# One attention-and-MLP kernel: TensorE's order fixed in the attention steps, maxima in own columns, every third step's scores in the ring of sums

## Chip, core and metric

The kernel runs on one core of a Trainium2 chip. The metric is the device time of one execution in microseconds (us); the median of several runs is given. TensorE multiplies matrices, VectorE, ScalarE and GpSimd work elementwise or along rows, SyncE issues transfers. Matrix products land in PSUM, eight banks in which each tile here fills one or part of one.

## The reference

The attention with random features, whose sizes are batch 8, heads 8, tokens 576, head width 64, 128 features:

```python
def phi(x):
    proj = np.einsum('bhsd,md->bhsm', x, omega)
    sq = np.sum(x * x, axis=-1, keepdims=True) / 2.0
    h = proj - sq
    h = h - np.max(h, axis=-1, keepdims=True)
    return np.exp(h) / np.sqrt(m)
q_p, k_p = (phi(q_s), phi(k_s))
kv = np.einsum('bhsm,bhsd->bhmd', k_p, v)
z = np.sum(k_p, axis=2)
num = np.einsum('bhsm,bhmd->bhsd', q_p, kv)
den = np.einsum('bhsm,bhm->bhs', q_p, z)[..., None] + 1e-06
return (num / den).astype(np.float32)
```

Its output, heads side by side, is the input x of a token mixing `u = x + (xT @ U @ V)T` and of an MLP `u + relu(u @ w_ch1) @ w_ch2` with widths 512 and 2048.

## The kernel before

**Attention.** The work is cut into 16 units, each two batches by two heads, and a unit's tokens into 9 tiles of 128. A round works on the keys of one unit and on the queries of an earlier one (both of its parts are queries or keys at the ends), and a round has 9 steps, one for each tile. A step goes through stages that are spread over the loop's passes (`DELAY`): 2 passes after its start it is projected, at 3 its maxima are taken, at 4 the exponentials run and are used, at 5 the transposed exponentials are copied out of PSUM, at 6 the query products are made, at 7 the result is divided. So in each pass TensorE meets stages of several steps. These are:

- **Projection** (`Step.project`): six matmuls, three for each part, into a bank of scores `p_p`. The ring `p_p` has two banks, so that step n+2 writes where step n was.
- **Maxima** (`peak`): one reduction on VectorE over the four score blocks, into a small tile `nm` of a ring of two.
- **Exponentials** (`exp`): four on ScalarE, with `nm` as the bias, first the two of the queries (`exp1`), then the two of the keys, into `e`, a ring of two.
- **Key product** (`Keys.use`): two products of `e` with the values, added up over the round in a bank `p_kv` or `p_m`.
- **Transposition** (`Queries.use`): two, of the queries' `e` against the identity, into `p_q`, a ring of two; `copy` moves them to `eT` on VectorE or ScalarE in turn.
- **Query product** (`Queries.combine`): two products of `eT` with the finished `kv`, into a tile of sums `p_n`, a ring of two banks. A tile holds two steps (step 4 has one alone). In `finish`, VectorE adds the small constant (L603), takes reciprocals (L604) and multiplies (L618), after which the slot is free.

Once per four units a mixer (`mixing`) puts its matmuls `py` and `ph` between these, and now and then a piece of a weight (`decoding`) or of the MLP's input (`ahead`) is prepared.

**What sets the order.** The kernel is recorded in program order and a scheduler then orders each engine's instructions by modelled times. Instructions inside `tc.keep_in_program_order(...)` keep their order among themselves on their engine. Before, in the attention steps these are on TensorE the key products

```python
tc.keep_in_program_order(nc.tensor.matmul(
    o, e[:, j, :], w, start=(s == 0 and j == 0), stop=(s == NT - 1), skip_group_check=True
))
```

while projections, transpositions and query products (`nc.tensor.matmul(...)` alone) go where the scheduler puts them. Everything after the attention steps, the MLP, is kept in program order.

## Time and profile before

| | |
|---|---|
| median of 3 runs | 1040.44 us (1040.01 to 1041.32) |
| profiled execution | 1040.75 us |
| its span, first to last instruction | 1039.0 us |
| TensorE matmuls, weight loads busy | 1030.3, 988.6 us |
| VectorE, ScalarE, GpSimd busy | 780.7, 588.7, 464.9 us |
| granted TensorE clock, mean | 0.999 |

The table is of the profiled execution but for its first line. A matmul's end is modelled and its time overlaps with that of the next; weight loads, which run one ahead of the matmuls, are a row of their own (PEld). The starts of weight loads tell best how long a piece of TensorE's work takes.

### The profile page before, as it was taken

To read this page: it belongs to the slowest core of one execution; us is meant where nothing else is said; L and a number is where in the kernel's file an instruction comes from. 1 tells how busy PE (TensorE), PEld (TensorE's weight loads), DVE (VectorE), ACT (ScalarE), POOL (GpSimd) and SP (SyncE) were. 2 spreads that over 40 slices of the span, in tenths; PEclk is the share of its full clock that TensorE was granted. 3 is DMA by queue.
4 is the path that set the end of the run, shared out by engine and by line. 5 is a ranking of instruction groups with operands and counts; after the bars stand their busy time and mean duration, and the time that the engine had idled before them with its cause. 6 is when DMAs were issued, how large, how long until landed. Compare 5 with 4: busy or idle time off the path is not lost.

```text
span 1039.0 us, 19292 instructions
## 1 busy us (share of the span) xinstructions
PE 1030.3 (99%) x6487; PEld 988.6 (95%) x6487; DVE 780.7 (75%) x1549; ACT 588.7 (57%) x1481; POOL 464.9 (45%) x419
## 2 busy tenths in 40 slices
PE   9999999999999999999999999999999999999998
PEld 7999999999989999999898999999999999999998
DVE  3898998998987776487678666886678676875556
ACT  4989889899865654454443534543455334543441
POOL 2356547567344654578773423322333223322231
PEclk9999999999999999999999999999999999999999
DMA  6899889788315474389868999989999899889887
GB/s 153 149 170 147 164 177 169 166 172 139 97 51 171 145 177 77 112 276 300 285 241 278 309 294 303 282 270 281 288 277 284 270 287 277 270 261 273 262 235 181
DMA packets 372883, 226.44 MB, mean 218 GB/s; under 512 B 307760, under 2 KB 324912, under 8 KB 372784
## 3 DMA queue, kind: packets, MB, share of 16 engines
q1 hardware_dynamic: 369712, 224.26, 80.3%
q10 hardware_dynamic: 3072, 0.95, 0.4%
q8 instruction: 52, 0.85, 0.4%
q14 instruction: 47, 0.39, 0.1%
HBM read 176.91 MB, written 48.23 MB: 217 GB/s over the span
## 4 chain that ended last, share of the span: by engine, by line
PE 82%; DVE 2%; DMA 1%; ACT 1%; POOL 0%; issue 0%; DVEq 0%; POOLq 0%; ACTq 0%
PE p_s L1124 27%; PE p_c L1414 12%; PE p_o L1414 6%; PE p_p L1095 6%; PE p_n L1247 4%; PE p_q L1247 4%; PE p_r L1414 3%; PE p_n L593 3%; PE p_kv L479 2%; PE p_kv L1247 2%; PE p_m L1247 2%; PE p_p L635 2%; PE p_q L573 2%; PE p_p L636 2%; PE p_p L637 2%; PE py L338 1%
## 5 line engine op out<-in xcount | busy, mean ns | idle before, releaser
L1124 PE MATMUL p_s<-ux,wx 128*128 128x384 f32 x1680 | 332.3, 335 | 0.2 <-ACT near L1194 0.2
L1124 PEld LDWEIGHTS p_s<-ux,wx 128*128 128x128 f32 x1680 | 295.7, 188 | 4.0 <-ACT near L1194 0.7
L650 ACT ACTIVATE e<-p_p,nm 128x128 f32<-128x128 f32 x540 | 156.8, 389 | 22.1 <-DVE nm L643 11.7
L905 POOL TENSOR_TENSOR near<-b,near 128x384 f32<-128x384 f32 x32 | 42.3, 1323 | 263.3 <-DVE near L1173 247.7
L1414 PE MATMUL p_c<-t,wy 128*128 128x384 f32 x756 | 151.1, 334 | 0.3 <-DMA wy<-w2x_dram 0.3
L1414 PEld LDWEIGHTS p_c<-t,wy 128*128 128x128 f32 x756 | 132.8, 188 | 0.6 <-DMA wy<-w2x_dram 0.6
L428 POOL TENSOR_TENSOR xl<-xT,xh 128x384 fp32r<-128x384 f32 x90 | 91.5, 1038 | 83.9 <-ACT xh L424 58.0
L643 DVE TENSOR_REDUCE nm<-p_p 128x4 f32<-128x512 f32 x135 | 91.9, 681 | 15.4 <-PE p_p L637 8.2
L635 PE MATMUL p_p<-omh,xh 128*128 128x256 f32 x270 | 85.9, 318 | 0.6 <-ACT e L650 0.6
L905 DVE TENSOR_TENSOR near<-p_s,near 128x384 f32<-128x384 f32 x88 | 48.8, 555 | 48.5 <-PE p_s L1124 42.2
L905 POOL TENSOR_TENSOR t<-near,t 128x768 fp32r<-128x768 f32 x32 | 59.3, 1853 | 41.0 <-ACT t L1183 41.0
L1414 PE MATMUL p_o<-t,wy 128*128 128x384 f32 x384 | 76.9, 334 | 0.0
L637 PE MATMUL p_p<-omh,xl 128*128 128x256 f32 x270 | 75.8, 281 | 0.0
L636 PE MATMUL p_p<-oml,xh 128*128 128x256 f32 x270 | 75.8, 281 | 0.0
L593 PE MATMUL p_n<-kv,eT 128*128 128x65 f32 x512 | 71.1, 268 | 0.1
L593 PEld LDWEIGHTS p_n<-kv,eT 128*128 128x128 f32 x512 | 67.1, 192 | 2.4 <-DVE eT L578 0.4
L1414 PEld LDWEIGHTS p_o<-t,wy 128*128 128x128 f32 x384 | 67.5, 188 | 0.0
L1095 PE MATMUL p_p<-ux,wx 128*128 128x384 f32 x360 | 66.4, 335 | 0.0
L905 DVE TENSOR_TENSOR w1f<-p_c,w1f 128x384 f32<-128x384 f32 x78 | 43.4, 557 | 29.8 <-PE p_c L1414 29.5
L1095 PEld LDWEIGHTS p_p<-ux,wx 128*128 128x128 f32 x360 | 63.4, 188 | 1.5
L573 PE MATMUL p_q<-ident,e 128*128 128x128 f32 x288 | 60.5, 277 | 0.8 <-ACT e L650 0.7
L479 PE MATMUL p_kv<-vt,e 128*128 128x65 f32 x416 | 57.6, 261 | 0.0
(202 smaller groups left out, 2263.1 us busy)
## 6 DMA issues: line engine op xcount, KB each, us to landing
wx<-wx_dram SPq DMA_DIRECT2D x112, 512.0 KB, 4.5
wy<-w2x_dram SPq DMA_DIRECT2D x112, 512.0 KB, 5.0
raw<-in_moe_w_ch_dram SPq DMA_DIRECT2D x32, 512.0 KB, 4.1
wx_dram<-wx SPq DMA_DIRECT2D x56, 256.0 KB, 2.6
u_dram<-x SPq DMA_DIRECT2D x36, 256.0 KB, 2.3
qt<-in_q_dram SPq DMA_DIRECT2D x120, 72.0 KB, 3.0
uraw<-u_dram SPq DMA_DIRECT2D x80, 96.0 KB, 5.4
kt<-in_k_dram SPq DMA_DIRECT2D x52, 144.0 KB, 4.8
```

The lines of the kernel that those rows point to most:

```text
L428: rest.tensor_tensor(out=self.xl[-1], in0=self.turned, in1=f32(self.xh[-1]), op=ALU.subtract)
L593: nc.tensor.matmul(pn[:, h, :], eT[:, h, :], kv[:, h, s // 5, :], start=True, stop=True)
L635: nc.tensor.matmul(o, part.xh[g][:, ts], oh, start=True, stop=False)
L636: nc.tensor.matmul(o, part.xh[g][:, ts], ol, start=False, stop=False)
L637: nc.tensor.matmul(o, part.xl[g][:, ts], oh, start=False, stop=True)
L643: nc.vector.tensor_reduce(out=self.nm[:, :n], in_=self.pp[:, :n], axis=AX.X, op=ALU.max, negate=True)
L650: nc.scalar.activation(out=self.e[:, j, :], in_=self.pp[:, j, :], func=AF.Exp, bias=self.nm[:, j : j + 1])
L905: keep(engine.tensor_tensor(out=out, in0=a, in1=b, op=op))
L1095: keep(nc.tensor.matmul(ph, l, r, start=(cc + i == 0), stop=(cc == NC - 1 and i == 2)))
L1124: keep(nc.tensor.matmul(o, l, r, start=(i in (0, 1, 3) and k + j == 0), stop=(k == 1 and j == 2), skip_group_check=True,))
L1247: keep(nc.tensor.matmul(po, l, r, start=(begin and n + i == 0), stop=(end and n == len(fs) - 1 and i == 2)))
L1414: keep(nc.tensor.matmul(bank, l, r, start=(fresh and n + m == 0), stop=(n == 1 and m == 2), skip_group_check=True,))
```

## The change

Three things. First, the key products, the transpositions and the query products of a pass become generators, whose instructions are drawn in the order `KTKTUU`: a key product (K), a transposition (T), again K and T, then the two query products (U). Each is kept in program order, up to the steps of the last two rounds, where none of the three kinds is kept any longer (before, the key products were kept everywhere). Projections stay free. Second, the four maxima of each step go to four columns of the first weight tile `w1f`, other columns for each step, instead of into the ring `nm`. Third, every third projected step takes its bank of scores from the ring `p_n` in place of `p_p`; both rings still have two banks.

```diff
@@ class Keys, FirstKeys: use
-                tc.keep_in_program_order(nc.tensor.matmul(
+                yield nc.tensor.matmul(
                     o, e[:, j, :], w, start=(s == 0 and j == 0), stop=(s == NT - 1), skip_group_check=True
-                ))
+                )
@@ class Queries: use, combine
+            self.pq[s] = pq
             for j in range(2):
-                nc.tensor.transpose(pq[:, j, :], e[:, j, :], ident)
-            self.pq[s] = pq
+                yield nc.tensor.transpose(pq[:, j, :], e[:, j, :], ident)
...
-                nc.tensor.matmul(pn[:, h, :], eT[:, h, :], kv[:, h, s // 5, :], start=True, stop=True)
+                yield nc.tensor.matmul(pn[:, h, :], eT[:, h, :], kv[:, h, s // 5, :], start=True, stop=True)
@@ class Step
         def project(self):
-            self.pp = ps.tile([P, 4, P], F32, name="p_p", tag="p_p", bufs=2)
+            projected[0] += 1
+            tag = "p_n" if projected[0] % 3 == 0 else "p_p"
+            self.pp = ps.tile([P, 4, P], F32, name="p_p", tag=tag, bufs=2)
...
-            self.nm = wk.tile([P, 4], F32, name="nm")
+            self.nm = w1f[:, NC - 1, DF // 2 + 4 * self.at : DF // 2 + 4 * self.at + 4]
@@ the loop over the steps
-        if at("use1") and at("use1").n > 1:
-            at("use1").use(1)
         if at("project"):
             at("project").project()
...
-        if at("use0"):
-            at("use0").use(0)
+        ops = {"K": [], "T": [], "U": []}
+        st = at("use0")
+        for i, p in enumerate(st.parts if st else []):
+            ops["T" if isinstance(p, Queries) else "K"].append(st.use(i))
+        st = at("combine")
+        ops["U"] += [p.combine(st.s) for p in st.queries()] if st else []
+        for kind in ORDER * 2:
+            while ops[kind]:
+                step = next(ops[kind][0], None)
+                if step is not None:
+                    if s < (NR - 2) * NT + DELAY["use0"]:
+                        tc.keep_in_program_order(step)
+                    break
+                ops[kind].pop(0)
```

What this makes of the order is seen at two places. The numbers in the names are those of buffers; `vt` and `vm` are values, `vm` those of step 4. The first place is on TensorE, a step in the middle of a round: before, the two key products, the two query products, the two transpositions, then the next projection.

```order
L479 MATMUL p_kv_2076<-vt1_113,e_2081 128x65 x2
L593 MATMUL p_n_2154<-kv_1716,eT_2123 128x65 x2
L573 MATMUL p_q_2139<-ident_78,e_2116 128x128 x2
L635 MATMUL p_p_2142<-omh_106,xh_2023 128x256
L636 MATMUL p_p_2142<-oml_107,xh_2023 128x256
L637 MATMUL p_p_2142<-omh_106,xl_2058 128x256
```

After, such a step reads:

```order
L479 MATMUL p_kv_1694<-vt0_111,e_1778 128x65
L574 MATMUL p_q_1806<-ident_78,e_1778 128x128
L479 MATMUL p_kv_1694<-vt0_111,e_1778 128x65
L574 MATMUL p_q_1806<-ident_78,e_1778 128x128
L593 MATMUL p_n_1774<-kv_1365,eT_1743 128x65 x2
L637 MATMUL p_p_1834<-omh_106,xh_1755 128x256
```

Each transposition now stands behind a key product, and the query products end the group.

The second place is the ring of sums, near the middle of a round. On TensorE before, the last products on the tile `p_n_2222` are followed by the first on `p_n_2307`, which takes the other slot: that of `p_n_2154`, whose last product stands some 30 rows further up.

```order
L637 MATMUL p_p_2210<-omh_106,xl_2171 128x256
L479 MATMUL p_kv_2076<-vm1_114,e_2187 128x2x65 x2
L593 MATMUL p_n_2222<-kv_1716,eT_2193 128x65 x2
L573 MATMUL p_q_2246<-ident_78,e_2221 128x128 x2
L586 MATMUL p_n_2307<-kv_1716,eT_2234 128x130 x2
```

After, `p_n_2169` takes the slot of `p_n_2103`, since between them the scores `p_p_2124` took the other slot, and its first product comes a few rows behind the last one on `p_n_2103`:

```order
L593 MATMUL p_n_2103<-kv_1679,eT_2075 128x65 x2
L479 MATMUL p_kv_2027<-vm1_114,e_2139 128x2x65
L574 MATMUL p_q_2165<-ident_78,e_2139 128x128
L479 MATMUL p_kv_2027<-vm1_114,e_2139 128x2x65
L574 MATMUL p_q_2165<-ident_78,e_2139 128x128
L312 MATMUL ph_2108<-y_1722,sv_109 128x512
L479 MATMUL p_kv_2027<-vt1_113,e_2173 128x65
L574 MATMUL p_q_2203<-ident_78,e_2173 128x128
L593 MATMUL p_n_2169<-kv_1679,eT_2110 128x65 x2
```

The distance from a slot's last product to its next use has shrunk from some 30 rows to 7. On VectorE, what frees the slot is the product that reads `p_n_2154` before and `p_n_2103` after. Before:

```order
L603 TENSOR_SCALAR rec_2197<-p_n_2154 128x4
L578 COPY eT_2159<-p_q_2139 128x256
L643 TENSOR_REDUCE nm_2185<-p_p_2142 128x4
L604 RECIPROCAL rec_2197<-rec_2197 128x4
L315 TENSOR_TENSOR x_572<-ph_2157,x_572 128x512
L618 TENSOR_TENSOR x_1825<-p_n_2154,rec_2197 128x2x128
```

After:

```order
L603 TENSOR_SCALAR rec_2147<-p_n_2103 128x4
L604 RECIPROCAL rec_2147<-rec_2147 128x4
L578 COPY eT_2183<-p_q_2165 128x256
L420 STREAM_TRANSPOSE xT_2185<-qt_1892 128x384
L618 TENSOR_TENSOR x_1785<-p_n_2103,rec_2147 128x2x128
```

The reduction that stood between reciprocal and product has gone elsewhere; in its place there are a copy of the transposition `p_q_2165` and a transposition of queries (L420).

## Rows read from the trace of the kernel before

**Rows 1.** The page: span, and busy time and instructions of each engine.
```profile
span 1039.0 us, 19292 instructions
...
PE 1030.3 (99%) x6487; PEld 988.6 (95%) x6487; DVE 780.7 (75%) x1549; ACT 588.7 (57%) x1481; POOL 464.9 (45%) x419
```

**Rows 2.** Stretches: us, busy us (instructions) of PE, PEld, DVE, ACT, POOL, clock, DMA share, GB/s.
```profile
27.32:295.13 267.81, 265.84 (x2239) 256.64 (x2239) 240.96 (x606) 241.16 (x779) 152.31 (x142) 1.00 0.80 150
...
312.00:1039.00 727.00, 722.51 (x3977) 696.35 (x3975) 514.85 (x878) 324.87 (x636) 298.00 (x245) 1.00 0.84 249
```

**Rows 3.** Stretches of one round (nine steps) each, columns as above.
```profile
150.33:167.47 17.14, 17.14 (x151) 16.91 (x151) 15.89 (x42) 16.73 (x54) 11.57 (x11) 1.00 0.90 166
188.25:206.72 18.47, 17.89 (x149) 16.92 (x147) 18.25 (x47) 16.35 (x53) 9.59 (x9) 1.00 0.79 182
```

**Rows 4.** Timeline, weight loads of two steps: start us, us from first to last end.
```profile
57.69 0.53 PEld L479 LDWEIGHTS p_kv<-vt,e 128*128 128x128 f32 x4
58.08 0.20 PEld L573 LDWEIGHTS p_q<-ident,e 128*128 128x128 f32 x1
58.19 0.53 PEld L593 LDWEIGHTS p_n<-kv,eT 128*128 128x128 f32 x4
58.59 0.20 PEld L573 LDWEIGHTS p_q<-ident,e 128*128 128x128 f32 x1
58.70 0.20 PEld L635 LDWEIGHTS p_p<-omh,xh 128*128 128x128 f32 x1
...
59.41 0.53 PEld L479 LDWEIGHTS p_kv<-vt,e 128*128 128x128 f32 x4
59.81 0.26 PEld L573 LDWEIGHTS p_q<-ident,e 128*128 128x128 f32 x2
60.03 0.53 PEld L593 LDWEIGHTS p_n<-kv,eT 128*128 128x128 f32 x4
60.48 0.19 PEld L635 LDWEIGHTS p_p<-omh,xh 128*128 128x128 f32 x1
```

**Rows 5.** Timeline, weight loads of another step.
```profile
48.63 0.53 PEld L479 LDWEIGHTS p_kv<-vt,e 128*128 128x128 f32 x4
49.08 0.53 PEld L593 LDWEIGHTS p_n<-kv,eT 128*128 128x128 f32 x4
```

**Rows 6.** Waits from 27 to 295 us: us in total, times, longest.
```profile
DVE nm L643 <- ACT e L650: 3.3, 8, 0.9
...
PEld p_p L635 <- ACT e L650: 2.4, 9, 0.4
...
PEld p_q L573 <- ACT e L650: 1.0, 2, 0.5
...
PE p_q L573 <- ACT e L650: 0.7, 2, 0.4
...
PE p_p L635 <- ACT e L650: 0.6, 3, 0.2
```

**Rows 7.** VectorE's groups from 27 to 295 us: busy us, mean ns; idle before.
```profile
L578 DVE COPY eT<-p_q 128x256 f32<-128x256 f32 x76 | 31.2, 411 | 3.2 <-PE p_q L573 2.2
...
L420 DVE STREAM_TRANSPOSE xT<-qt 128x384 f32<-128x384 f32 x44 | 23.9, 544 | 0.0
```

**Rows 8.** Timeline of VectorE, two tiles of sums on their way out.
```profile
123.79 0.15 DVE L603 TENSOR_SCALAR rec<-p_n 128x4 f32<-128x4 f32 x1
...
125.44 0.41 DVE L618 TENSOR_TENSOR x<-p_n,rec 128x256 f32<-128x256 f32 x1
...
242.02 0.12 DVE L603 TENSOR_SCALAR rec<-p_n 128x4 f32<-128x4 f32 x1
...
242.39 0.42 DVE L618 TENSOR_TENSOR x<-p_n,rec 128x256 f32<-128x256 f32 x1
```

**Rows 9.** Timeline of TensorE, two mixing matmuls that follow each other.
```profile
295.93 0.40 PE L338 MATMUL py<-ml,su 128*128 128x512 f32 x1
296.16 0.40 PE L338 MATMUL py<-mh,su 128*128 128x512 f32 x1
```

More of the change, by code (lines that the diff above doesn't have):

```diff
@@ L533, in use @@
                     o, w = self.acc[:, h, j], self.v[:, j, 5 * h + t + i, :]
-                tc.keep_in_program_order(nc.tensor.matmul(
+                yield nc.tensor.matmul(
                     o, e[:, i, :], w, start=(s == 0 and i == 0), stop=(s == NT - 1), skip_group_check=True
-                ))
+                )
         def turn(self):
@@ L553, in low @@
             pass
-    shared = {}
+    shared, projected = {}, [0]
     class Queries(Part):
@@ L585, in combine @@
                 for h in range(2):
-                    nc.tensor.matmul(self.mixed[:, h], eT[:, h, :], kv[:, h], start=True, stop=True)
+                    yield nc.tensor.matmul(self.mixed[:, h], eT[:, h, :], kv[:, h], start=True, stop=True)
                 return
@@ L622, in performer_mlp_kernel, with __init__ @@
     class Step:
-        def __init__(self, parts, s):
-            self.parts, self.s, self.n = parts, s, len(parts)
+        def __init__(self, parts, s, at):
+            self.parts, self.s, self.n, self.at = parts, s, len(parts), at
         def project(self):
-            self.pp = ps.tile([P, 4, P], F32, name="p_p", tag="p_p", bufs=2)
+            projected[0] += 1
+            tag = "p_n" if projected[0] % 3 == 0 else "p_p"
+            self.pp = ps.tile([P, 4, P], F32, name="p_p", tag=tag, bufs=2)
             oh, ol = omh.rearrange("p j m -> p (j m)"), oml.rearrange("p j m -> p (j m)")
@@ L663, in use @@
         def use(self, i):
-            self.parts[i].use(self.s, self.e[:, 2 * i : 2 * i + 2, :])
+            return self.parts[i].use(self.s, self.e[:, 2 * i : 2 * i + 2, :])
     class FirstStep(Step):
@@ L754, in performer_mlp_kernel @@
     AFTER, LATE = 91, 15
+    ORDER = "KTKTUU"
     first_wx = []
@@ L779, in performer_mlp_kernel @@
         if r < NR:
-            steps[s] = (Step if r else FirstStep)(rounds[r], t)
+            steps[s] = (Step if r else FirstStep)(rounds[r], t, s)
         if r + 1 < NR:
@@ L862, in performer_mlp_kernel @@
                 split_omega()
-        st = at("combine")
-        for p in st.queries() if st else []:
-            p.combine(st.s)
         if mixers:
```

## The prediction

> **What bounds the kernel now.** I began with the page's share of busy time: TensorE holds 99% of the span [rows 1]. The stretches then split the span into three [rows 2]. From 27.3 to 295.1 us, the attention steps that the change touches, TensorE's matmuls are busy 265.8 of 267.8 us, its weight loads 256.6, VectorE 241.0 and ScalarE 241.2. From 312 us on, TensorE is busy 722.5 of 727.0 us with an order that the change leaves alone. The granted clock is 1.00 in both, the 2.4 GHz level. So whatever the attention stretch gains or loses arrives at the end unchanged, and what it can gain is limited: weight loads fill 96% of it, the two other engines 90%. Single rounds have less room [rows 3]: in the one from 188.25 us VectorE is busy 18.25 of 18.47 us, in the one from 150.33 us ScalarE 16.73 of 17.14. A TensorE saving of half a microsecond a round therefore fits into the stretch as a whole, though not into every round.
>
> **The order: what a transposition costs.** Each fp32 product is two weight loads in the trace, so a pair of key products or of query products is a group of four loads, and a transposition is one. Read the starts of the loads [rows 4]. In the step from 57.69 us each transposition stands alone behind a product: from the key products' first load to the next projection's 58.70 - 57.69 = 1.01 us pass. In the next step, from 59.41 us, the same work has its two transpositions side by side: 60.48 - 59.41 = 1.07 us. The missing time is in the products: four loads take 0.45 us when another product or a projection follows [rows 4, 5] and 0.39 to 0.40 when a transposition follows, whichever product it is. A transposition adds about 0.11 us either way. So each transposition that stands behind a product instead of behind another transposition saves 0.05 to 0.06 us; I take 0.055. Counted through both programs' orders, 125 of the 288 transpositions stand behind a product before, 239 after: 114 more, 114 x 0.055 = **6.3 us saved**. Before shows no transposition directly ahead of a key product; it shows one ahead of query products, whose loads have the same shape [rows 4], so I take the same price. If the key product's first load paid the 0.055 back, the term would be 0; that is its other bound.
>
> A rule speaks against this term. The Trainium skill, "TensorE: Matmul & The Clock Gate", section on LDWEIGHTS, has a weight load's time follow its number of columns alone, about 107 ns for 128; every load here has 128, so by that rule no order is cheaper than another and the term would be 0 in place of 6.3. This trace differs from it: 1.01 against 1.07 us for the same loads.
>
> **The third bank of scores.** Before, the scores of step n+2 take the bank of step n, so the projection waits for all four exponentials of step n; the transpositions wait for their own. TensorE's waits for the exponentials [rows 6] are 2.4 + 0.6 us at the projections and 1.0 + 0.7 at the transpositions, 4.7 in all. With each third step's scores elsewhere, a projection in the scores' own ring follows the exponentials of the step three before. I take two thirds of the projections' 3.0 as gone: **2.0 us saved**, bounds 0 and 3.0. The transpositions' 1.7 I leave: their key product now stands ahead of them and waits for a later exponential, though further behind its projection. As the bound of a gain I keep it.
>
> **The ring of sums.** This ring has two slots and gets 3 more tiles a round beside its 5. A slot that held sums is free once VectorE has done its adding, reciprocal and product on it. That takes 0.79 us when the three stand together (242.02 to 242.81 [rows 8]) and 2.06 when reductions and copies stand between (123.79 to 125.85 [rows 8]). Before, a slot's next tile opens so late that TensorE never shows a wait for it. After, I counted TensorE's work between a slot's last product and its next use along the new order, with 0.118 us a projection matmul, 0.225 a product, 0.055 more for a transposition behind it (all from the load starts in [rows 4]), 0.23 a mixing matmul [rows 9]: 78 hand-overs, 27 of them with less than 2.06 us, the shortest 1.0. The piece quoted with the change is one: between the last product on p_n_2103 and the first on p_n_2169 lies 1.08 us, and VectorE's product that frees the slot stands behind a copy of the transposition p_q_2165, which comes only 0.5 us ahead, and one of VectorE's own transpositions (L420). Copy, transposition and product take 0.41, 0.54 and 0.42 us [rows 7, 8]; TensorE must stand there for most of a microsecond, and the next key products and projections with it. Adding up VectorE's rows between the three operations, 8 of the 78 hand-overs fall short of their cover, by 7.4 us together. The bounds are 0 (VectorE's rows overlap at their ends, and a stall at one place lengthens the cover of the next) and, if also the other short ones take 2.06 us, 12.6. I take half of the 7.4: **3.7 us lost**.
>
> **Maxima in own columns.** The reduction no longer waits until the exponentials of two steps before have read the same four columns: 3.3 us of VectorE's waits [rows 6]. VectorE is not what ends TensorE's waits in most rounds, and [rows 6] show none of TensorE's waits ended by a reduction. I count 0, and 3.3 as the bound of a gain. No instruction is added or taken away on any engine, and no DMA moves for it. The columns lie in a part of the first weight tile that is decoded after the attention steps.
>
> **The sum.** -6.3 - 2.0 + 3.7 = -4.6 us. Against the profiled execution, 1040.75 us (span 1039.0 and 1.75 around it), that is 1036.15; the median of the three runs is 0.31 lower. I forecast **1036 us**. A measurement of this kernel can tell about 0.2%, 2.1 us, from no change: under 1038.4 is faster, over 1042.5 slower.
>
> **The rivals.**
> - *The ring costs nothing and the exponentials' waits all go*: -6.3 - 4.7 = -11.0, 1029.5 us. For it: key products stand on average 4 us behind their projection in the new order, transpositions before 2.7. Against it: p_n_2169, and the rounds in which VectorE or ScalarE is full [rows 3].
> - *The order is worth nothing*, because a product pays back behind a transposition what it gave ahead of it: -2.0 + 3.7 = +1.7, 1042 us, within the 0.2%. Against it stand the 1.01 and 1.07 us; for it, that no row shows a key product behind a transposition. By the skill's rule on weight loads this is the case.
> - *The ring of sums decides*: slower. Place: the query product that opens a tile in a slot which VectorE has not yet freed; it is kept in order, so key products, transpositions and the exponentials of later steps queue behind it. Price: the 12.6 us at 27 places, 1040.4 - 8.3 + 12.6 = 1045 us. It decides from 10.4 us of ring waits on, 0.39 us at each of the 27.
>
> **How the numbers follow.** The forecast's case 57% (its own range 1032.5 to 1039), ring free 15%, order worth nothing 11%, ring decides 17%. Faster: most of the first and all of the second, 68%; within 0.2%: the rest of the first and the third, 15%; slower 17%. A range that leaves out no more than 2 in 10 reaches down to near the second case and up past the third: 1030 to 1043 us.
>
> **What would show it.** Right: in the stretch of attention steps, which ends 4 to 5 us earlier, four loads ahead of a transposition still take 0.39 to 0.40 us in groups of two with 0.11 behind; TensorE's rows show no wait for exponentials at projections, and new waits at the query products for VectorE's product on p_n. Wrong: loads of the key product behind a transposition that start 0.05 us later than behind a projection (order worth nothing); waits of query products that sum to over 10 us (ring decides); or VectorE above 95% busy in all rounds, which would cap the gain before TensorE's saving is used.

## The result, and the profile after

The changed kernel takes 1046.57 us (median of 6 runs, 1043.38 to 1048.90), the kernel before 1040.22 (median of 6). The ratio is 1.0053, 95% interval 1.0037 to 1.0069: about 6 us slower. I had forecast 1036 us, with 1043 as the upper end. The direction is wrong.

The profiled execution took 1043.43 us, one of the shortest. Over both runs of this kernel (f1_after_again is the second), the five executions with a mean granted clock of 0.999 or 1.000 took 1042.9 to 1046.0 us, the six with 0.997 or 0.998 took 1046.1 to 1048.9; the kernel before, run beside the experiments, never lies under 0.999. So about 3 of the 6 us go with a lower clock in executions that no profile shows. The profiles below show shorter ones.

The page of the profiled execution, span and first part:

```profile
span 1041.6 us, 19160 instructions
PE 1027.4 (99%) x6487; PEld 985.0 (95%) x6487; DVE 784.6 (75%) x1549; ACT 584.5 (56%) x1481; POOL 465.4 (45%) x419
```

The two stretches that answer to [rows 2] (busy us of PE, PEld, DVE, ACT, POOL; clock; DMA share; GB/s):

```profile
27.32:295.13 267.81, 261.07 (x2223) 251.70 (x2221) 242.59 (x601) 235.03 (x774) 149.95 (x140) 1.00 0.82 150
312.00:1039.00 727.00, 725.36 (x3993) 699.36 (x3991) 517.25 (x881) 326.01 (x639) 298.77 (x245) 1.00 0.84 249
```

In the attention stretch TensorE's matmuls are busy 4.8 us less than before and its weight loads 4.9 us less. Not all of that is saved: 18 weight loads fewer lie in the stretch, some 2 us at 0.115 us each (an estimate from the starts in [rows 4]), and come later instead. The rest is the cheaper order. But the work is not done earlier; TensorE stands more. The waits of the changed kernel from 27 to 295 us (total us, times, longest) say for whom, and answer to [rows 6]:

```profile
ACT eT L578 <- PE p_q L574: 14.7, 11, 2.8
DVE w1f L645 <- PE p_p L639: 11.8, 24, 1.4
...
PEld p_p L637 <- ACT e L652: 3.8, 8, 1.2
...
PEld ph L312 <- DVE x L315: 3.3, 4, 1.3
...
PEld p_kv L479 <- ACT e L652: 1.3, 3, 0.6
...
PE p_p L637 <- DVE rec L603: 1.0, 1, 1.0
...
PE p_p L637 <- DVE x L618: 0.8, 3, 0.4
```

A matmul and its weight load can show the same wait, so one of the two rows is to be read, not their sum. VectorE's reductions no longer wait for exponentials (3.3 us in [rows 6]). TensorE's waits for exponentials have not gone, though, and three others are new or have grown: for mixing's bank (`ph`, 3.3 us, 0.6 before), for the sums' ring (1.0 + 0.8 us at projections, none at query products), and those of ScalarE's copies, which stand 14.7 us (3.1 before) in front of transpositions not yet made. One such place, on ScalarE and then on TensorE:

```profile
139.74 1.21 ACT L652 ACTIVATE e<-p_p,w1f 128x128 f32<-128x128 f32 x4
143.79 0.37 ACT L578 COPY eT<-p_q 128x256 f32<-128x256 f32 x1 [2.84 <-PE p_q L574]
144.06 1.15 ACT L652 ACTIVATE e<-p_p,w1f 128x128 f32<-128x128 f32 x4
```

```profile
141.00 0.39 PE L637 MATMUL p_p<-omh,xh 128*128 128x256 f32 x1 [0.38 <-ACT e L652]
...
142.91 0.28 PE L639 MATMUL p_p<-omh,xl 128*128 128x256 f32 x1
143.02 0.33 PE L479 MATMUL p_kv<-vt,e 128*128 128x65 f32 x2
143.19 0.28 PE L574 MATMUL p_q<-ident,e 128*128 128x128 f32 x1
```

From 141.00 to 143.02 TensorE does projections of more than one step in a row, as the third bank lets the planner. No transposition is made in that time; the copy waits 2.84 us for one, and the next four exponentials stand behind the copy. Ten projection matmuls or more (a step has six, and a few records are missing) stand in a row, mixing aside, at 23 places of the changed kernel's trace, at 1 before.

The loads themselves came out as priced. The weight loads of a step in the new order:

```profile
142.91 0.30 PEld L479 LDWEIGHTS p_kv<-vt,e 128*128 128x128 f32 x2
143.09 0.19 PEld L574 LDWEIGHTS p_q<-ident,e 128*128 128x128 f32 x1
143.19 0.31 PEld L479 LDWEIGHTS p_kv<-vt,e 128*128 128x128 f32 x2
143.37 0.20 PEld L574 LDWEIGHTS p_q<-ident,e 128*128 128x128 f32 x1
143.48 0.42 PEld L593 LDWEIGHTS p_n<-kv,eT 128*128 128x128 f32 x3
```

Four loads of key products and two transpositions take 143.48 - 142.91 = 0.57 us, as against 60.03 - 59.41 = 0.62 in [rows 4]. Over the trace, a load ahead of a transposition is followed after 58 ns (median of 216), one behind a transposition after 110 ns. The load after that, the product's second, comes 115 to 116 ns later, in place of 110 to 111 before: about 5 of the 53 ns are paid back. The rule of the Trainium skill ("TensorE: Matmul & The Clock Gate", section on LDWEIGHTS), one price for loads of one width, does not hold here; the measurement decides.

Last comes the end of the attention. TensorE in the kernel before, then in the changed kernel, from the last product of the last mixing's first half (`py<-ml`) to the first MLP product (`p_p<-ux,wx`):

```profile
299.46 0.48 PE L338 MATMUL py<-ml,su 128*128 128x512 f32 x1
299.77 0.60 PE L573 MATMUL p_q<-ident,e 128*128 128x128 f32 x4
300.21 1.90 PE L593 MATMUL p_n<-kv,eT 128*128 128x65 f32 x16
302.18 0.50 PE L338 MATMUL py<-mh,su 128*128 128x512 f32 x1
...
303.23 1.22 PE L1095 MATMUL p_p<-ux,wx 128*128 128x384 f32 x6
```

```profile
303.26 0.48 PE L338 MATMUL py<-ml,su 128*128 128x512 f32 x1
303.57 1.00 PE L593 MATMUL p_n<-kv,eT 128*128 128x65 f32 x8
305.13 0.50 PE L338 MATMUL py<-mh,su 128*128 128x512 f32 x1 [0.55 <-DVE y L345]
...
306.16 1.03 PE L1105 MATMUL p_p<-ux,wx 128*128 128x384 f32 x5
```

The second half waits for ScalarE's and VectorE's work on the first half's bank. Before, 4 transpositions and 16 matmuls of query products stand between and cover all of that; after, 8 matmuls do, and TensorE stands 0.55 us. This does not make the end longer: from the first half to the second it is 2.7 us before and 1.9 after. What does lies ahead of the two. The last reduction starts at 297.1 us in both kernels; from there to the first MLP product TensorE loads weights 28 times for query products, 8 for transpositions and 7 for mixing before, 36, 10 and 10 times after. Of the 2.9 us more, 1.9 are such loads, work that before stood ahead of the last reduction, and 1.1 are standing (split as in the next section).

### The profile page after: what moved, and what is told of

It is laid out like the page before. It is cut to its first block, busy times and chain, and to the rows that moved or that the text cites. A ratio compares the mean times of both kernels' runs of the same rounds, so it can differ in the third digit from the quotient of the medians.

```text
span 1041.6 us, 19160 instructions
## 1 busy us (share of the span) xinstructions
PE 1027.4 (99%) x6487; PEld 985.0 (95%) x6487; DVE 784.6 (75%) x1549; ACT 584.5 (56%) x1481; POOL 465.4 (45%) x419
## 4 chain that ended last, share of the span: by engine, by line
PE 87%; DVE 7%; ACT 3%; issue 1%; SPq 1%; POOL 1%; DMA 0%; DVEq 0%; ACTq 0%; POOLq 0%
PE p_s L1134 27%; PE p_c L1424 12%; PE p_o L1424 6%; PE p_p L1105 6%; PE p_n L1257 4%; PE p_q L1257 4%; PE p_r L1424 3%; PE p_n L593 3%; PE p_kv L479 3%; PE p_p L637 2%; DVE w1f L645 2%; PE p_kv L1257 2%; PE p_m L1257 2%; PE p_p L639 2%; PE p_p L638 2%; PE p_q L574 2%
## 5 line engine op out<-in xcount | busy, mean ns | idle before, releaser
L652 ACT ACTIVATE e<-p_p,w1f 128x128 f32<-128x128 f32 x540 | 159.8, 425 | 16.6 <-DVE w1f L645 9.8
L915 POOL TENSOR_TENSOR near<-b,near 128x384 f32<-128x384 f32 x32 | 42.4, 1324 | 262.6 <-DVE near L1183 247.0
L645 DVE TENSOR_REDUCE w1f<-p_p 128x4 f32<-128x512 f32 x135 | 90.5, 680 | 14.4 <-PE p_p L639 13.5
L915 DVE TENSOR_TENSOR near<-p_s,near 128x384 f32<-128x384 f32 x88 | 48.8, 555 | 49.2 <-PE p_s L1134 42.5
L639 PE MATMUL p_p<-omh,xl 128*128 128x256 f32 x270 | 78.4, 292 | 0.0
L574 PE MATMUL p_q<-ident,e 128*128 128x128 f32 x288 | 75.1, 278 | 0.0
L479 PE MATMUL p_kv<-vt,e 128*128 128x65 f32 x416 | 66.8, 253 | 0.3 <-ACT e L652 0.3
```

What stands on the lines that cost most here:

```text
L479: yield nc.tensor.matmul(o, e[:, j, :], w, start=(s == 0 and j == 0), stop=(s == NT - 1), skip_group_check=True)
L639: nc.tensor.matmul(o, part.xl[g][:, ts], oh, start=False, stop=True)
L645: nc.vector.tensor_reduce(out=self.nm[:, :n], in_=self.pp[:, :n], axis=AX.X, op=ALU.max, negate=True)
L652: nc.scalar.activation(out=self.e[:, j, :], in_=self.pp[:, j, :], func=AF.Exp, bias=self.nm[:, j : j + 1])
L915: keep(engine.tensor_tensor(out=out, in0=a, in1=b, op=op))
```

## The experiments

In the table, "steps" runs from the start of the tenth reduction to that of the last, "end" from there to the first MLP product, both read from the timelines. The steps are split by the starts of TensorE's weight loads: where the time between two starts is over 0.12 us longer than the median for that pair of operations in the same trace, the excess is "standing", all else "loads". How finely the pairs are told apart moves this split by about 1 us. Work can move from the steps to the end, so their sum tells more than either. The first line is the kernel before; run again beside each group of runs its median was 1040.1 to 1041.3 us, and ratios and differences to before are to that.

| run | median us | ratio to before (95%) | steps = loads + standing | end |
|---|---|---|---|---|
| before | 1040.22 | | 252.4 = 242.2 + 10.2 | 6.2 |
| changed | 1046.57 | 1.0053 (1.0037-1.0069) | 253.5 = 238.5 + 15.0 | 9.1 |
| e1_order | 1042.80 | 1.0026 (1.0013-1.0039) | 251.4 = 237.7 + 13.7 | 9.4 |
| e2_bank | 1043.62 | 1.0032 (1.0021-1.0043) | 253.0 = 242.9 + 10.1 | 10.0 |
| e3_maxima | 1040.46 | 1.0004 (0.9996-1.0013) | 252.2 = 242.4 + 9.7 | 6.1 |
| e4_order_maxima | 1043.61 | 1.0035 (1.0023-1.0048) | 251.4 = 236.9 + 14.5 | 9.5 |
| e5_ahead | 1042.01 | 1.0011 (1.0001-1.0021) | 253.2 = 238.5 + 14.8 | 6.5 |
| e5b_adjacent | 1047.97 | 1.0066 (1.0053-1.0079) | 259.8 = 247.0 + 12.8 | 6.9 |
| e6_ahead_bank | 1052.49 | 1.0105 (1.0090-1.0121) | 263.6 = 240.0 + 23.6 | 6.6 |
| e7_keepall | 1046.33 | 1.0050 (1.0037-1.0064) | 254.3 = 239.9 + 14.4 | 9.6 |
| e8_before_2exp | 1037.68 | 0.9970 (0.9960-0.9981) | 248.5 = 241.7 + 6.8 | 7.3 |
| e9_order_2exp | 1037.18 | 0.9964 (0.9951-0.9976) | 247.5 = 236.3 + 11.2 | 8.7 |
| e10_after_2exp | 1045.24 | 1.0039 (1.0026-1.0053) | 254.5 = 240.4 + 14.1 | 8.4 |
| e11_bank_pq | 1041.24 | 1.0000 (0.9991-1.0009) | 253.2 = 241.3 + 12.0 | 6.6 |
| f1_after_again | 1046.08 | 1.0054 (1.0041-1.0067) | 253.6 = 238.9 + 14.7 | 9.1 |
| f2_pq_held | 1047.73 | 1.0070 (1.0057-1.0082) | 257.4 = 241.3 + 16.1 | 6.6 |
| f3_ahead_pq_held | 1046.64 | 1.0063 (1.0048-1.0078) | 258.0 = 237.4 + 20.6 | 5.6 |
| f4_ufree | 1044.46 | 1.0033 (1.0021-1.0045) | 253.9 = 236.7 + 17.2 | 6.3 |
| g1_before_light | 1034.81 | 0.9947 (0.9932-0.9962) | 246.3 = 241.9 + 4.4 | 6.6 |
| g2_order_light | 1031.99 | 0.9919 (0.9905-0.9933) | 244.6 = 238.2 + 6.4 | 6.6 |

**One part at a time.**

e1_order, the changed kernel without the other two parts:

```diff
-            tag = "p_n" if projected[0] % 3 == 0 else "p_p"
+            tag = "p_p"
-            self.nm = w1f[:, NC - 1, DF // 2 + 4 * self.at : DF // 2 + 4 * self.at + 4]
+            self.nm = wk.tile([P, 4], F32, name="nm")
```

> The fixed order alone on the kernel before; scores and maxima stay in their old rings. Theory L (lateness: a transposition behind a key product that waits for a later exponential comes late, its copy then blocks ScalarE's queue, and the exponentials behind it): the order itself carries the loss, 1042 to 1047 us, ScalarE's copies wait more than 10 us for transpositions in the attention steps (3.1 before, 15.9 after). Theory S (the sums' ring, with a third of the scores in it, carries the loss): the order alone keeps its saving, 1033 to 1038 us. Theory M (mixing's bank: TensorE stands at the mixing product for VectorE's adding, 1.0 us before, 5.8 after): 1039 to 1042 us, with these waits over 4 us.

Measured: 2.7 us slower than before. The loads of the steps fell by 4.5 us, standing rose by 3.5, and the end took 3.2 longer. As in the changed kernel, part of the end's growth is moved work: over steps and end together loads fell by 3.0 to 3.5 us and standing rose by 5.4 to 5.8, 2.2 us more in all. TensorE's longest wait from 27 to 295 us, and ScalarE's for the reductions behind it:

```profile
ACT e L652 <- DVE nm L645: 15.6, 33, 1.3
...
PEld p_p L637 <- ACT e L652: 9.9, 21, 1.2
```

The projections wait for exponentials 9.9 us, 2.4 in [rows 6]. ScalarE's copies waited only 7.3 us for transpositions, under the 10 that theory L gave, and mixing's bank 1.0: the time fits L, its mechanism only in part, and M fails.

e2_bank, the kernel before with the one line:

```diff
-            self.pp = ps.tile([P, 4, P], F32, name="p_p", tag="p_p", bufs=2)
+            projected[0] += 1
+            tag = "p_n" if projected[0] % 3 == 0 else "p_p"
+            self.pp = ps.tile([P, 4, P], F32, name="p_p", tag=tag, bufs=2)
```

> The third bank of scores alone on the kernel before, order and maxima as before. Theory L: no loss, since the transpositions are not moved: 1038 to 1041 us. Theory S: a loss, 1043 to 1048 us, with TensorE's waits at query products for VectorE's product on the sums over 5 us. My forecast's terms (-2.0 at the projections, up to +3.7 at the ring): 1038 to 1042 us.

Measured: 3.6 us slower, as S has it, but not for S's reason: no wait of a query product for VectorE's product on the sums shows. With more banks the free planner put 81 transpositions behind a projection and 42 behind a product (before 4 and 121), and such loads lie in pairs again:

```profile
100.26 0.19 PEld L639 LDWEIGHTS p_p<-omh,xl 128*128 128x128 f32 x1
100.39 0.25 PEld L573 LDWEIGHTS p_q<-ident,e 128*128 128x128 f32 x2
100.61 0.53 PEld L479 LDWEIGHTS p_kv<-vt,e 128*128 128x128 f32 x4
```

The loads from the tenth reduction to the first MLP product grew by 3.4 us; 79 transpositions at 0.055 us would be 4.3. Much of this came due at the end (10.0 us).

e3_maxima, the kernel before with the maxima in the weight tile's columns:

```diff
-            self.nm = wk.tile([P, 4], F32, name="nm")
+            self.nm = w1f[:, NC - 1, DF // 2 + 4 * self.at : DF // 2 + 4 * self.at + 4]
```

> The maxima in columns of their own alone on the kernel before. My forecast's term: 0, so 1039 to 1041 us, with VectorE's wait for the exponentials at the reduction (3.3 us before) gone. A rival: reductions that no longer wait come earlier in VectorE's queue and hold up what frees a bank behind them: over 1042 us.

Measured: no difference. My 0 holds.

e4_order_maxima, the changed kernel with all scores in their own ring:

```diff
-            tag = "p_n" if projected[0] % 3 == 0 else "p_p"
+            tag = "p_p"
```

> The changed kernel with all scores in their own ring again, that is the fixed order and the maxima in own columns. Theory L: as slow as the changed kernel or slower, 1044 to 1048 us. Theory S: 1032 to 1038 us, since only the bank was to blame. If order and bank are bad only together: this and the bank alone both at 1036 to 1041 us.

Measured: 3.5 us slower than before, 0.4 us under the range that L gave. The changed kernel is 3.0 us slower by medians, 1.7 in steps and end together: that is the bank's price in the written order. The other 1.3 us lie outside them, and the changed kernel has more executions at a lower clock (six of 11, here two of six).

**Which order, and whether any.**

e5_ahead, on e1_order: query products and transpositions alternate ahead of the projection, key products follow it.

```diff
+        issue("UTUT")
         if at("project"):
             at("project").project()
-        for kind in ORDER * 2:
-            ...
+        issue("KK")
```

> The fixed order alone (old rings), but another one: a step's query products and transpositions alternate ahead of the next projection, and its key products stand behind that. 215 of 288 transpositions stand behind a product, as against 245 in the run with the order alone and 130 before. Theory L (in the fixed order the projection stands ahead of the transpositions, so it waits for all four exponentials of the step with everything behind it; 15.3 us there, 3.0 before): these waits fall under 7 us, the saving of the loads shows, 1034 to 1038 us. Rival F (any fixed order takes from the planner the freedom to fill such waits): they stay over 10 us, 1041 to 1045 us. Theory E (the loss of the order alone lies at the end of the attention, where the last mixing's second half stands for VectorE with no transposition or product left to cover it): here two microseconds of such work stand between the halves, so the time from the last reduction to the first MLP product is back at 6 to 7 us (9.4 with the order alone), worth 2 to 3 us whatever the projections do.

Measured: 0.7 us slower than before. The end is back at 6.5 us, as E has it. The projections' waits for exponentials fell to 4.8 us (L), but the transpositions wait now (2.2 us on the loads' row) and the standing in the steps is no less. Saved loads: 3.7 us. So L's detail, what stands ahead of the projection, only moves the waits.

e5b_adjacent, the same with the calls

```diff
-        issue("UTUT")
+        issue("TT")
-        issue("KK")
+        issue("KKUU")
```

> As the run before in this list, but a step's two transpositions side by side ahead of the projection and key and query products behind it: 80 of 288 transpositions behind a product in place of 215. If a transposition behind a product saves 0.055 us also where the order is fixed and TensorE is the bound, this run is 5 to 7 us slower than the one with query products and transpositions in turn. If waits for other engines take up what the loads save, under 2 us lie between the two.

Measured: 6.0 us slower than e5_ahead, for 135 transpositions fewer behind a product, 0.044 us each. Loads 8.5 us longer, standing 2 less. The price is real and reaches the measured time when it is *added*. By the rule of the Trainium skill on weight loads ("TensorE: Matmul & The Clock Gate", section on LDWEIGHTS) the two would be equal.

e6_ahead_bank, e5_ahead with

```diff
-            tag = "p_p"
+            tag = "p_n" if projected[0] % 3 == 0 else "p_p"
```

> The order with the transpositions ahead of the projection, with each third step's scores in the ring of sums. Theory S+ (order and bank are only bad together, since in the fixed order a late slot of the sums' ring holds everything behind it): slower than the same order with the old rings by 2 to 6 us. My forecast's terms for the bank (up to 3 gained, up to 3.7 lost): within 2 us of it.

Measured: 10.5 us slower than e5_ahead, more than any theory gave. Standing rose by 8.8 us, 3.8 of it at projections and 2.7 at key products. Again ten or more projection matmuls stand in a row, at 19 places. Up to 1.7 us of the standing can be the clock's (an estimate: half of 3.4 us): in this profile the granted clock is 0.50, the 1.2 GHz level, from 47.6 to 51.1 us, after TensorE has stood 1.2 us for VectorE's product on the sums. The other three executions, at a mean of 1.000, took as long, so the 10.5 us are not the clock's.

e7_keepall, the changed kernel with

```diff
-                    if s < (NR - 2) * NT + DELAY["use0"]:
-                        tc.keep_in_program_order(step)
+                    tc.keep_in_program_order(step)
```

> The changed kernel with its order kept to the very end, the last units too. Theory E (loss at the end of the attention): eight query products then stand between the two halves of the last mixing in place of four, which gives 1 to 2 us back: 1043 to 1046 us by the median (1046.6 the changed kernel), and 7.5 to 8.5 us from the last reduction to the first MLP product (9.1). Theory S+: no change of more than 1 us, since the loss lies in the steps.

Measured: no difference from the changed kernel, and the end as long (9.6 us). Cover between the two halves does not shorten it: here TensorE also stands ahead of them, 0.35 us for a copy and 0.48 for a split of the mixed rows. Over all runs the end goes with the work that the planner leaves behind the last reduction: 37 to 48 weight loads of query products, transpositions and mixing in ends of 5.6 to 6.9 us, 52 in the one of 7.3, 56 to 65 in those of 8.4 to 10.0. No run varied that placing alone.

**Relieving the other engines.** These kernels change the maxima, so their outputs differ.

e8_before_2exp, the kernel before with

```diff
-            for j in (2 * i, 2 * i + 1):
-                nc.scalar.activation(
-                    out=self.e[:, j, :], in_=self.pp[:, j, :], func=AF.Exp, bias=self.nm[:, j : j + 1]
-                )
+            j = 2 * i
+            nc.scalar.activation(
+                out=self.e[:, j : j + 2, :], in_=self.pp[:, j : j + 2, :], func=AF.Exp, bias=self.nm[:, j : j + 1]
+            )
```

> The kernel before with one exponential for both halves of a part in place of two, so two a step in place of four; both halves take the first half's maximum, so the scores' values and the output differ. ScalarE is relieved by some 50 us in the steps. It is the base for the next two. If ScalarE's exponentials end TensorE's waits before, 1033 to 1038 us; if TensorE's loads alone bound it, 1039 to 1041 us.

Measured: 3.2 us faster. ScalarE's exponentials did end waits of TensorE.

e9_order_2exp, e1_order with the same edit:

```diff
-            for j in (2 * i, 2 * i + 1):
+            j = 2 * i
...
```

> The order alone, with the same two exponentials a step. Theory W (the order's cheaper loads are real, 2 to 6 us, but on the kernel before they became waits for the exponentials at the projections): with ScalarE relieved the saving shows, 3 to 6 us below the kernel before with two exponentials, and the waits at the projections are under 5 us. Rival F (the fixed order makes waits of its own, whoever is late): no faster than the kernel before with two exponentials, or slower by up to 3 us, with the waits moved to VectorE's reduction or mixing's bank.

Measured: 0.5 us below e8_before_2exp, in the place of 2.7 above. The two intervals overlap, so this is no difference; W's saving did not come, though its other sign did, with waits of 4.4 us at the projections. ScalarE now waits 30.7 us for VectorE's reductions (15.6 in e1_order).

e10_after_2exp, the changed kernel with it:

```diff
-            for j in (2 * i, 2 * i + 1):
+            j = 2 * i
...
```

> The changed kernel with the same two exponentials a step. Theory W: the third bank is then without use, since no exponential is waited for; it is 0 to 3 us slower than the order with two exponentials. Theory S+ (the third step's scores in the sums' ring make waits of their own, for VectorE's adding and product, which a relieved ScalarE doesn't change): 2 to 5 us slower than it. If the bank was bad through ScalarE's queue alone: no slower, within 1 us.

Measured: 8.1 us slower than e9_order_2exp. The bank is bad also with ScalarE relieved. ScalarE's copies wait twice as long for transpositions (12.7 us in e9_order_2exp), and ten projection matmuls or more stand in a row at 32 places:

```profile
ACT eT L578 <- PE p_q L574: 26.4, 21, 2.6
```

e11_bank_pq, the changed kernel with

```diff
-            tag = "p_n" if projected[0] % 3 == 0 else "p_p"
+            tag = "p_q" if projected[0] % 3 == 0 else "p_p"
```

> The changed kernel with each third step's scores in the ring of the transposed weights in place of the ring of sums. Theory S+ (the ring of sums is the wrong place, since its slots come free late, after an adding, a reciprocal and a product on VectorE): 1 to 4 us faster than the changed kernel, as that ring is freed by one copy. Rival: each transposition then waits for the copy of the one before, in a ring that has one slot left while scores hold the other: 5 us slower or more than the changed kernel.

Measured: as fast as before, 5 us better than the changed kernel: the ring of sums was the worse place. In the steps the two rings cost the same (0.3 us apart); the profiles show 2.5 of the 5 us at the end. The rest they do not show, but all 11 executions here have a mean clock of 0.999 or more, of the changed kernel's only five of 11. Ten projection matmuls or more stand in a row here too, at 14 places.

f1_after_again, the changed kernel unchanged:

> The changed kernel once more, on the chip of the runs beside it, since its profiled execution (1043.4 us) lies 3 us below its median (1046.6). If the difference is chance outside the steps (when the granted clock rises in the first 14 us, and the wait for the weights' transfers near 600 us), this profile differs from the first in these two places and by under 1 us between the tenth reduction and the first MLP product (262.6 us); if the steps themselves vary, by more.

Measured: from the tenth reduction to the first MLP product the two profiles are within 0.2 us (262.6 and 262.7), so the steps do not vary between them. Both profiled executions lie at the low end (1042.9 and 1043.4). Over all runs two other places vary: the tenth reduction starts at 42.5 to 46.6 us (43.1 and 43.5 in these two), and in the MLP, near 600 us, the first 60 weight loads for `t,wy`, among which TensorE waits for transfers of weights, take 27.0 to 29.6. What the record adds is the granted clock: the longer executions are those with a mean of 0.997 or 0.998. A mean lower by 0.002 to 0.003 is up to 2 or 3 us of 1045 (an estimate: at half the clock, half of that time is lost). None of these executions was profiled, so where the clock falls in them, and what else adds to the 3 us, is not shown.

f2_pq_held, e11_bank_pq with the projections kept in order:

```diff
+                held = tc.keep_in_program_order if self.at < (NR - 2) * NT else lambda step: step
-                nc.tensor.matmul(o, part.xh[g][:, ts], oh, start=True, stop=False)
+                held(nc.tensor.matmul(o, part.xh[g][:, ts], oh, start=True, stop=False))
```

> The changed kernel with each third step's scores in the ring of the transposed weights, and the projections kept in the written order too, so that 222 transpositions again stand behind a product (187 without that, since projections had slid between). At 0.055 us each that is 2 us below the run with that ring alone: 1038 to 1040 us. If projections that may not slide wait for their bank with everything behind them: 1041 to 1045 us.

Measured: 7.4 us slower than before. The transpositions wait, for exponentials and for copies (from 27 to 295 us):

```profile
PEld p_q L574 <- ACT e L653: 5.7, 11, 0.8
...
PEld p_q L574 <- DVE eT L578: 2.9, 7, 0.8
```

f3_ahead_pq_held, the order of e5_ahead with that ring, own columns for the maxima and the projections held:

```diff
-            tag = "p_p"
+            tag = "p_q" if projected[0] % 3 == 0 else "p_p"
```

> Query products and transpositions in turn ahead of the projection, key products behind it, the third step's scores in the ring of the transposed weights, projections kept in order. It joins the order that gave the fewest waits at the end of the attention with the ring that did not hold up the sums. If the two add up, 1037 to 1040 us. If each transposition, now ahead of the projection, waits for the copy of the one before, 1043 us or more.

Measured: 6.3 us slower. Few loads (237.4), the best end (5.6), and 20.6 us of standing.

f4_ufree, e1_order with the query products left to the planner:

```diff
-                    if s < (NR - 2) * NT + DELAY["use0"]:
+                    if kind != "U" and s < (NR - 2) * NT + DELAY["use0"]:
```

> The order alone, but with the query products left to the planner; key products and transpositions alternate as written, 236 transpositions behind a product. Rival F (what is fixed can't fill the projections' waits; query products are what the planner would fill them with): the projections' waits for exponentials fall below 5 us (9.9 on the weight loads' row with all three fixed) and the time to 1036 to 1040 us. If the waits are those of scores in two banks whatever stands between: unchanged, 1041 to 1044 us.

Measured: 4.2 us slower than before; the projections wait 8.5 us, nearly as with all three fixed. Rival F fails: the freed query products did not fill these waits, and wait 3.4 us themselves for copies of transpositions (0.4 before).

g1_before_light, e8_before_2exp with

```diff
-                out=self.nm[:, :n], in_=self.pp[:, :n], axis=AX.X, op=ALU.max, negate=True
+                out=self.nm[:, :n], in_=self.pp[:, :n, : P // 2], axis=AX.X, op=ALU.max, negate=True
```

> The kernel before with ScalarE and VectorE both relieved: two exponentials a step in place of four, and a reduction that looks at half of each score's columns in place of all (maxima and output differ). VectorE's reduction, 0.68 us with 512 columns, is then near 0.37, some 38 us less in the steps. It is the base of the next run. If VectorE bounded the steps beside TensorE: 1031 to 1036 us; if TensorE's loads alone, as the run with two exponentials: 1037 to 1038 us.

Measured: 5.5 us below before, in the range for VectorE as a bound beside TensorE.

g2_order_light, e9_order_2exp with the same line:

```diff
-                out=self.nm[:, :n], in_=self.pp[:, :n], axis=AX.X, op=ALU.max, negate=True
+                out=self.nm[:, :n], in_=self.pp[:, :n, : P // 2], axis=AX.X, op=ALU.max, negate=True
```

> The order alone with the same two edits. Theory W (the cheaper loads are real and were given back because VectorE and ScalarE, 90 per cent busy, answer a projection no sooner): 3 to 6 us faster than the kernel before with these edits, and TensorE's waits in the steps no longer than there. Rival F (the written order makes waits of its own, whoever is late): within 1.5 us of it or slower, with the waits at the projections still 4 us or more longer.

Measured: 2.8 us faster than g1_before_light, just short of W's 3. Against W, TensorE still stands 2.0 us more in the steps; against F, the projections wait only 2.4 us longer. Their waits for exponentials from 27 to 295 us, e8_before_2exp and e9_order_2exp first, then the two light kernels:

```profile
PEld p_p L635 <- ACT e L650: 1.1, 5, 0.4
```

```profile
PEld p_p L637 <- ACT e L652: 4.4, 8, 1.1
```

```profile
PEld p_p L635 <- ACT e L650: 0.2, 1, 0.2
```

```profile
PEld p_p L637 <- ACT e L652: 2.6, 3, 1.0
```

The stretch from 45 to 295 us of either, columns as in [rows 2], g1_before_light first:

```profile
45.00:295.00 250.00, 249.63 (x2125) 243.56 (x2125) 205.63 (x588) 192.66 (x483) 147.31 (x138) 1.00 0.78 150
```

```profile
45.00:295.00 250.00, 248.15 (x2146) 242.08 (x2145) 210.34 (x597) 195.71 (x485) 151.54 (x139) 1.00 0.83 150
```

With VectorE at 82 to 84% and ScalarE at 77 to 78%, of the order's 3.7 us of loads in the steps 1.7 come through, and the end is equal.

So by medians the order is worth +2.7, -0.5, -2.8 us as first ScalarE and then VectorE are relieved, and +2.2, +0.4, -1.7 in steps and end together. The loads saved there are much the same (3.0 to 3.5 us with neither engine relieved, 3.1 to 3.7 with both). The standing that the order adds falls from between 5.4 and 5.8 us to between 1.4 and 2.0; with ScalarE alone relieved the split is less certain, 2.8 to 5.2. It is the engines that must answer which were changed. One thing besides them differs: the planner orders the free instructions anew. With the old order 121, 99 and 98 transpositions stand behind a product, with the new one 227, 222 and 220, so up to 1 us of the swing (at 0.055 us each) may be the planner's.

## Why the prediction was wrong

**The step that failed** is the first part's "A TensorE saving of half a microsecond a round therefore fits into the stretch as a whole". I read 90% on VectorE and ScalarE as room. A projection needs its reduction and four exponentials before its bank is free, and each stands in a queue of an engine that is busy 9 parts in 10; when TensorE comes sooner, it meets the bank still in use. The run with the order alone shows it: from the tenth reduction to the first MLP product 3.0 to 3.5 us of loads were saved and 5.4 to 5.8 us of standing added. The relieved pairs show the reason: with both engines lightened the added standing is 1.4 to 2.0 us and the saving arrives.

**The order, -6.3.** The price of one transposition was nearly right: 58 against 110 to 117 ns, about 5 ns paid back, and 0.044 us each in the measured time of e5b_adjacent against e5_ahead. In the order alone, 106 more of them behind a product (227 in the trace, 121 before) would be 5.8 us; 3.0 to 3.5 came as loads, and why not more is not shown. Standing, for which this part of the sum had no term, took all of it and 2.2 us more. As it stood in the sum the term is +2.7.

**The third bank, -2.0 and +3.7 for its ring.** The sum of the two, +1.7, has the right sign by luck; the bank measures +3.0 in the written order, 1.7 of it in steps and end. Neither half is right. The gain was read from the old order, whose waits were small (and I added the rows of PE and of the weight loads, which show one wait twice: 3.4 us, not 4.7); in the new order 10.4 us of projections' waits (e4_order_maxima) fell to 3.8. The loss did not come where I put it: no query product waits for VectorE's product from 27 to 295 us, and the ring's waits are 1.8 us at projections. What came is what the planner does with a third bank, projections in a row with the transpositions late behind them. That is read from the trace and from its 23 and 32 places; no run held the projections with this ring, so it is not tested by itself. Two runs speak against it as the whole cause: e11_bank_pq has such rows at 14 places and is as fast as before, and f2_pq_held, with the projections held in that ring, has one such place, as the kernel before, and is 7.4 us slower than it. What makes the bank's price stays open.

**Maxima, 0.** Right.

**The rivals.** "The ring of sums decides" gave 1045 us, near the result, by another mechanism: its 27 query products do not wait. "The order is worth nothing" is nearer in spirit, though products pay back only about a tenth. What would have pointed there were the single rounds [rows 3], where VectorE or ScalarE is full; I let the mean over the stretch outvote them.

**What would show it.** The cheap loads appeared. The stretch did not end 4 to 5 us earlier: the last reduction starts at 297.1 us in both. The new waits stood elsewhere than at the query products. The cap by the answering engines came without the sign that I named for it: VectorE is 91% busy in the stretch, not above 95%.

## What to carry to other kernels

A busy share of 99% on one engine is no proof that it alone sets the pace: here, where a ring of two banks ties it to two engines at 90%, time saved on it turned into waits at the ring, while time added to it still counted for the most part. Before pricing a cheaper order, relieve the answering engines in a trial kernel and see whether the saving appears. And where a planner orders the rest, an added buffer is also a licence to reorder: look at what it now puts in a row and who waits meanwhile, up to the end of the stage.

## What the runs showed of the hardware

A transposition whose weight load stands behind an fp32 product starts its load 58 ns after the product's last one, in place of 110 to 117 ns behind another transposition. Little is paid back behind it: 110 ns to the next key product's first load, then 115 to 116 to its second (110 to 111 before). Behind a projection a transposition's load takes 133 ns (81 cases in e2_bank).

In e6_ahead_bank, for 3.4 us at the 1.2 GHz level (granted clock 0.50), the weight loads of a projection start 0.21 us apart, in place of 0.118 at the 2.4 GHz level.
